# A fused attention, feed-forward and expert kernel: k and v loaded a chunk ahead, second group of their products in block 7; in the first chunk root and Relu read PSUM and the constants are made there; the last chunk's counts in block 9

## The chip, the cores and the metric

The kernel runs on one core of a Trainium2 chip. TensorE (PE in the rows) multiplies, VectorE (DVE), ScalarE (ACT) and GpSimd (POOL) work on elements, and SyncE (SP) issues most of the DMAs. Each engine works through its own queue in order, and engines wait for one another by semaphores. The metric is the device time in us of one execution, the median over runs.

## The reference

Three stages in float32. Attention without a softmax on q, k and v of (8 batches, 8 heads, 576 tokens, 64), a feed-forward layer 512 to 2048 to 512 with a leaky Relu (a slope alpha for each of the 2048 features), and a mixture of 8 experts (512 to 1024 to 512) of which each of the 4608 tokens takes one:

```python
kv = einsum('bhsd,bhse->bhde', k, v)
out = einsum('bhsd,bhde->bhse', q, kv)
x = out / sqrt(mean(out*out, -1) + 1e-6) * g_norm     # then tokens x 512
h = x @ w_in
x = (maximum(h, 0) + alpha * minimum(h, 0)) @ w_out
logits = x @ w_gate + modality_bias[modality_id]      # 8 experts
e = argmax(logits);  gate = softmax(logits)[e]
out = gate * (maximum(x @ w1[e], 0) @ w2[e])
```

## The kernel before

Tokens go through the first two stages in 12 chunks (c) of 384 tokens; a chunk has 16 blocks (s), one for each 128 hidden features. Every operand of the large products is split into a high and a low part and three products are summed. In block s TensorE does `first(c, s)` (12 products, h of block s into one of two PSUM banks), then `second(c, s - 1)` (9 products into the three banks of y). Between them lies the chain of a block: h is made into gg (a leaky Relu), ScalarE rounds gg to ghi, GpSimd subtracts and leaves glo, and `second` reads both. In chunk 0 gg is made by two Relus of ScalarE (L367, L368) and one VectorE operation (L369); there `cut` also splits the weights: ScalarE L162 and L184, VectorE L171 and L176, GpSimd's subtraction L185, two cuts in a block. In later chunks gg is two VectorE operations that read h in PSUM (L371, L372), and the time is used for the rest:

- the attention of the next chunk: a batch covers one and a half chunks. In chunks 0, 2, 3, 5, 6, 8 and 9 the next chunk needs a new batch; its k and v come in four parts, into two slots `kvt`, by `load_kv` on SP. `kv_mm` (L228) multiplies two parts in block 3 and two in block 6, `kv_evict` (L232 on ScalarE, then L233 on VectorE) copies the result to `kvbd`, `attend` uses it from block 8 on (9 in chunk 0). `rsqrt` is the root of the norm, by integer steps on VectorE (L302 to L309).
- the choice of expert for the chunk before: `dots` on VectorE (24 of them, spread over the blocks by DOTS, in the last chunk by LAST_DOTS), `choose`, whose last result is hb, `count` (two small products that read hb), `weigh`, `place`, `scatter` of the rows into DRAM.
- the split of the experts' weights into DRAM, a piece a block in blocks 0 to 11: `pre_hi` (ScalarE), `pre_lo` (GpSimd, L215), `pre_store` (SP, L219), `pre_load` (SP, L208).

After the last chunk's `place`, `leader` picks the expert with the most tokens, whose rows and weights are loaded first; then 41 tiles of 128 rows go through the experts, TensorE busy throughout. The order of the work is the order in which the code calls the functions; a queue never takes a later instruction first. `spare` and the pool of `other` are PSUM, `one` and `two` are SBUF.

Of the kernel before, what the change touches and what calls it, by code (L numbers as in the profile page):

```python
# [13 lines left out]
I32 = mybir.dt.int32  # L14
U32 = mybir.dt.uint32
AF = mybir.ActivationFunctionType
ALU = mybir.AluOpType
# [6 lines left out]
S = 576  # L24
E = 8
NB = 8
CT = 384
NCH = NTOK // CT
# [12 lines left out]
FAR = [(1, e) for e in range(E)] + [(2, 6), (2, 7)]  # L41
PLAIN = 3
EARLY = 4
KV_AT = (0, 1, 3, 4)
DOTS = (0, 2, 5, 8, 11, 14, 17, 20, 22, 24)
LAST_DOTS = (0, 2, 5, 8, 12, 15, 18, 21, 24)


@with_exitstack
def fused(ctx: ExitStack, tc, qT, kv, g2, wmoe, alpha, wgate, bias, modality, w12, out):  # L50
    nc = tc.nc
    V, A, G, PE, SP = nc.vector, nc.scalar, nc.gpsimd, nc.tensor, nc.sync
# [23 lines left out]
    nalpha = one.tile([128, NFB], F32, name="nalpha")  # L76
# [32 lines left out]
    def other(n=512):  # L109
        return (pools[1] if pools else ps_a).tile([128, n], F32, tag="a", name="a")  # L110
# [179 lines left out]
    def rsqrt(c, others=(), part=None):  # L290

        if part == 1:
            fill(rsqrt_t[c], others)
            return
        ms = ms_t[c]
        if c > 1:
            it = spare[:, 96:120].bitcast(I32)
        else:
            it = one.tile([128, 24], I32, tag="it", name="it")
        u = one.tile([128, 24], F32, tag="u", name="u")  # L300
        y = it.bitcast(F32)
        steps = [lambda: V.tensor_scalar(ms, ms, 1.0 / 64, 1e-6, ALU.mult, ALU.add),  # L302
                 lambda: V.tensor_single_scalar(it, ms.bitcast(I32), 1, ALU.logical_shift_right),
                 lambda: V.tensor_tensor(it, magic, it, ALU.subtract),
                 lambda: V.tensor_scalar(ms, ms, -0.5, None, ALU.mult)]
        for _ in range(3):
            steps += [lambda: V.tensor_tensor(u, y, ms, ALU.mult),
                      lambda: V.tensor_tensor(u, u, y, ALU.mult),
                      lambda: V.scalar_tensor_tensor(y, u, 1.5, y, ALU.add, ALU.mult)]  # L309
        ms_t[c] = y  # L310
        rsqrt_t[c] = steps[7:]
        fill(steps[:7] if part == 0 else steps, others)
# [44 lines left out]
    def first(c, fb, between=None):  # L357
        ps = bank(CT)

        steps = [(k, *p) for k in range(4) for p in ((0, xhi), (0, xlo), (2, xhi))]  # L360
        if c == fb == 0:
            steps.sort(key=lambda step: (step[1], step[2] is xlo))
        for i, (k, part, x) in enumerate(steps):
            PE.matmul(ps, w_at(fb, part)[:, k * 128:(k + 1) * 128], x[:, k, :], start=(i == 0), stop=(i == 11))  # L364
        gg = two.tile([128, CT], F32, tag="gg", name="gg")
        if c == 0:
            A.activation(gg, ps, AF.Relu)  # L367
            A.activation(pad[:, 0:CT], ps, AF.Relu, scale=-1.0)  # L368
            V.scalar_tensor_tensor(gg, pad[:, 0:CT], nalpha[:, fb:fb + 1], gg, ALU.mult, ALU.add)  # L369
        else:  # L370
            V.tensor_scalar(gg, ps, 0.0, alpha_sb[:, fb:fb + 1], ALU.min, ALU.mult)  # L371
            V.scalar_tensor_tensor(gg, ps, 0.0, gg, ALU.max, ALU.add)  # L372
        if between:
            between()
        ghi = two.tile([128, CT], F32R, tag="ghi", name="ghi")
        A.copy(ghi, gg)  # L376
        glo = two.tile([128, CT], F32R, tag="glo", name="glo")
        G.tensor_tensor(glo, gg, ghi.bitcast(F32), ALU.subtract)  # L378
        g_t[c, fb] = (ghi, glo)
# [385 lines left out]
    with tc.manual_schedule():  # L765
# [72 lines left out]

        for c in range(NCH):
            nxt = c + 1  # L840
            kvb = [b for b in range(NB) if nxt < NCH and (nxt * CT) // S <= b <= (nxt * CT + CT - 1) // S
                   and not (c * CT) // S <= b <= (c * CT + CT - 1) // S]
            for s in range(NFB):
                edge = s == NFB - 1
                between = None
                if edge and nxt < NCH:
                    between = lambda: [take_x(nxt, k) for k in range(2)]
                elif s == 0 and c > 0:
                    between = lambda: [second(c - 1, NFB - 1, (2,)), y_out(c - 1, 1), y_out(c - 1, 0)]
                if c == 0:  # L850
                    cut(between=lambda: first(c, s, between))
                else:
                    first(c, s, between)
                if c == 0:
                    later = []
                    cut(later if s in (AT + 3, AT + 4) else None)
                    if s in AHEAD:
                        cut()
                if s == 0 and c > 0:
                    y_out(c - 1, 2)  # L860
                n = (c - 1) * 12 + s
                if c > 0 and s < 12 and n < 128:
                    pre_hi(n)
                    pre_lo(n)
                    pre_store(n)
                    if n + 2 < 128:
                        pre_load(n + 2)
                if c == 1 and 2 <= s < 6:
                    constants(s - 2)
                if s > 0:  # L870
                    second(c, s - 1)
                if edge and nxt < NCH:
                    for k in range(2, 4):
                        take_x(nxt, k)
                    second(c, s, (0, 1))
                elif edge:
                    turn_rows(0)
                    second(c, s)

                if kvb and s in (3, 6):  # L880
                    kv_mm(kvb[0], s - 3 and 2)
                    kv_mm(kvb[0], (s - 3 and 2) + 1)
                if kvb and s in KV_AT:
                    load_kv(kvb[0], KV_AT.index(s))
                if kvb and s == 6:
                    kv_evict(kvb[0])
                if nxt < NCH:
                    at = AT if c == 0 else 8
                    if at < s <= at + 3:
                        squares(nxt, s - at - 1)  # L890
                    if at <= s < at + 3:
                        if s != at + 1:
                            attend(nxt, (0, 1) if s == at else (2,))
                        attended(nxt, s - at)
                    if s == 11 and nxt + 1 < NCH:
                        load_q(nxt + 1)
                    if c == 0 and s in (at + 3, at + 4):
                        rsqrt(nxt, later, s - at - 3)
                    if c > 0 and s == at + 3:
                        rsqrt(nxt)  # L900
                    if s == at + 4:
                        scale_x(nxt, 0)
                        scale_x(nxt, 1)
                        turn_x(nxt, 0)
                    if s == at + 5:
                        scale_x(nxt, 2)
                        turn_x(nxt, 1)
                        turn_x(nxt, 2)

                if c > 0:  # L910
                    at = LAST_DOTS if nxt == NCH else DOTS
                    if s + 1 < len(at):
                        dots(c - 1, at[s], at[s + 1])
                    end = len(at) - 2
                    if s == end:
                        choose(c - 1)
                    if s == end + 1:
                        count(c - 1)
                        weigh(c - 1)
                    if s == end + 2:  # L920
                        place(c - 1)
                        if nxt == NCH:
                            leader()
                            scatter(c - 1, range(3))
                    if nxt < NCH and end + 2 <= s < end + 5:
                        scatter(c - 1, [s - end - 2])
                    if nxt == NCH and s == 11:
                        load_rows(0)
                        load_expert(0, (0,))
                        load_rows(1)  # L930
                        load_rows(2)
                        load_expert(0, (1,))
                elif edge:
                    pre_load(0)
                    pre_load(1)
                    SP.dma_start(wg_sb.rearrange("p a b -> p (a b)"), wgate.rearrange("a b -> (a b)").partition_broadcast(128))
                    G.memset(pad, 0.0)
                    G.memset(pad[:, D + 1:D + 2].bitcast(I32), OOB)
                    for j in range(8):
                        SP.dma_start(xb[E * BUCKET + j * 128:E * BUCKET + (j + 1) * 128], pad)  # L940
# [107 lines left out]
```

## Time and profile before

| | us |
|---|---|
| median of 3 runs | 1377.96 (1376.11 to 1378.64) |
| the profiled execution | 1376.92 |
| its span, first to last instruction | 1375.3 |
| TensorE busy | 1343.8 (98%) |
| VectorE, GpSimd, ScalarE busy | 995.7, 666.6, 526.9 |

Chunk 0 lasts until 110.6 us, the chunks after it some 72 us each until 906, the experts from there to the end. A matmul's busy time is modelled, and matmuls are pipelined, so the share of TensorE is read together with its waits: a wait is the idle time in front of an instruction, put down to what released it. A timeline row merges equal instructions in a row, gives the start of the first, and in brackets the idle time before it.

### The profile page before, as it was taken

To read this page: it belongs to the slowest core of one execution; us is meant where nothing else is said; L and a number is where in the kernel's file an instruction comes from. 1 tells how busy PE (TensorE), PEld (TensorE's weight loads), DVE (VectorE), ACT (ScalarE), POOL (GpSimd) and SP (SyncE) were. 2 spreads that over 40 slices of the span, in tenths; PEclk is the share of its full clock that TensorE was granted. 3 is DMA by queue.
4 is the path that set the end of the run, shared out by engine and by line. 5 is a ranking of instruction groups with operands and counts; after the bars stand their busy time and mean duration, and the time that the engine had idled before them with its cause. 6 is when DMAs were issued, how large, how long until landed. Compare 5 with 4: busy or idle time off the path is not lost. (4 is left out here: it accounts for less than half of the span.)

```text
span 1375.3 us, 26710 instructions
## 1 busy us (share of the span) xinstructions
PE 1343.8 (98%) x8886; PEld 1155.8 (84%) x8886; DVE 995.7 (72%) x2204; ACT 526.9 (38%) x1147; POOL 666.6 (48%) x643
## 2 busy tenths in 40 slices
PE   8989999999999999999999999999999999999997
PEld 7778888889898888988888889888888888888886
DVE  5779877777877777877777787756666666666662
ACT  4773323232332323232333333143444445544442
POOL 2765655555655464746555565543333333333320
PEclk9999999999999999999999999999999999999999
DMA  8855645453536364446545353367511171637784
GB/s 287 293 186 163 221 153 187 164 197 130 193 137 232 116 232 159 163 160 218 174 164 200 120 194 106 123 253 252 178 52 52 51 288 49 244 102 304 302 325 168
DMA packets 88949, 250.69 MB, mean 182 GB/s; under 512 B 19245, under 2 KB 39213, under 8 KB 86640
## 3 DMA queue, kind: packets, MB, share of 16 engines
q1 hardware_dynamic: 77056, 220.82, 45.6%
q0 software_dynamic: 11760, 28.14, 6.2%
q8 instruction: 78, 1.28, 0.4%
q14 instruction: 55, 0.45, 0.1%
HBM read 158.69 MB, written 91.54 MB: 182 GB/s over the span
## 5 line engine op out<-in xcount | busy, mean ns | idle before, releaser
L364 PE MATMUL h<-xhi,W 128*128 128x384 f32 x1536 | 430.0, 341 | 1.3 <-POOL W L185 0.7
L378 POOL TENSOR_TENSOR glo<-gg,ghi 128x384 fp32r<-128x384 f32 x192 | 237.2, 1235 | 360.8 <-ACT ghi L376 341.7
L392 PE MATMUL y<-W,ghi 128*128 128x512 f32 x1152 | 300.5, 396 | 8.3 <-ACT ghi L376 7.4
L376 ACT CAST ghi<-gg 128x384 fp32r<-128x384 f32 x192 | 98.9, 515 | 517.5 <-DVE gg L372 219.4
L364 PEld LDWEIGHTS h<-xhi,W 128*128 128x128 f32 x1536 | 280.4, 188 | 12.4 <-ACT xhi L353 1.5
L364 PE MATMUL h<-xlo,W 128*128 128x384 f32 x768 | 257.9, 336 | 0.0
L392 PEld LDWEIGHTS y<-W,ghi 128*128 128x128 f32 x1152 | 213.8, 188 | 48.9 <-ACT ghi L376 12.7
L409 DVE CUSTOM_DVE_ANT_0 junk<-yrow,wg_sb 128x512 f32<-128x512 f32 x242 | 218.6, 903 | 8.7 <-ACT yrow L403 3.1
L654 PE MATMUL h<-W,xhi 128*128 (+1 forms) x656 | 206.4, 395 | 0.0
L654 PE MATMUL y<-W,hth 128*128 (+1 forms) x656 | 204.6, 393 | 1.3 <-DMA W<-wsp 1.0
L215 POOL TENSOR_TENSOR raw<-raw 128x512 f32<-128x512 f32 x128 | 197.9, 1546 | 0.2
L371 DVE TENSOR_SCALAR gg<-h,alpha_sb 128x384 f32<-128x384 f32 x176 | 108.2, 615 | 118.2 <-PE h L364 112.5
L731 POOL DMA_INDIRECT out_dram<-kvbd,tail x41 | 43.2, 1054 | 283.3 <-ACT kvbd L729 240.4
L392 PE MATMUL y<-W,glo 128*128 128x512 f32 x576 | 163.7, 393 | 0.0
L364 PEld LDWEIGHTS h<-xlo,W 128*128 128x128 f32 x768 | 144.3, 188 | 5.9 <-DVE xlo L354 0.2
L654 PEld LDWEIGHTS h<-W,xhi 128*128 128x128 f32 x656 | 122.7, 187 | 29.7
L654 PEld LDWEIGHTS y<-W,hth 128*128 128x128 f32 x656 | 123.0, 188 | 28.4 <-DVE lg L409 1.4
L654 PE MATMUL h<-W,xlo 128*128 (+1 forms) x328 | 129.2, 394 | 0.0
L392 PEld LDWEIGHTS y<-W,glo 128*128 128x128 f32 x576 | 108.3, 188 | 23.4 <-POOL glo L378 0.7
L654 PE MATMUL y<-W,htl 128*128 (+1 forms) x328 | 127.8, 390 | 0.0
L691 DVE TENSOR_SCALAR hh<-h 32x256 f32<-32x256 f32 x296 | 123.3, 416 | 4.6
L712 DVE TENSOR_TENSOR htl<-hh,hth 128x512 fp32r<-128x512 f32 x74 | 51.2, 692 | 100.1 <-ACT hth L711 100.1
(212 smaller groups left out, 1492.9 us busy)
## 6 DMA issues: line engine op xcount, KB each, us to landing
wsp<-raw SPq DMA_DIRECT2D x128, 512.0 KB, 3.0
W<-wsp SPq DMA_DIRECT2D x16, 4096.0 KB, 14.5
raw<-in_w_dram SPq DMA_DIRECT2D x128, 256.0 KB, 3.5
kvt<-in_kv_dram SPq DMA_DIRECT2D x30, 512.0 KB, 5.0
xs<-xb POOLq DMA_DIRECT2D x140, 64.0 KB, 2.5
raw<-in_wmoe_dram SPq DMA_DIRECT2D x17, 511.8 KB, 5.2
qT<-in_qT_dram SPq DMA_DIRECT2D x11, 768.0 KB, 7.9
wg_sb<-in_wmoe_dram SPq DMA_DIRECT2D x15, 511.8 KB, 5.8
```

The source lines that it names most:

```text
L215: G.tensor_tensor(lo, lo, hi, ALU.subtract)
L364: PE.matmul(ps, w_at(fb, part)[:, k * 128:(k + 1) * 128], x[:, k, :], start=(i == 0), stop=(i == 11))
L371: V.tensor_scalar(gg, ps, 0.0, alpha_sb[:, fb:fb + 1], ALU.min, ALU.mult)
L376: A.copy(ghi, gg)
L378: G.tensor_tensor(glo, gg, ghi.bitcast(F32), ALU.subtract)
L392: PE.matmul(y_t[c][t], a[:, t * 128:(t + 1) * 128], w, start=(fb == i == 0), stop=(fb == NFB - 1 and i == 2))
L409: V.tensor_tensor_reduce(spare if i >= 22 else junk, y, wg_sb[:, e, :], 1.0, 0.0, ALU.mult, ALU.add, lg_t[c][:, t, e:e + 1])
L654: m = PE.matmul(ps, a, w, start=start, stop=stop)
L691: m = V.tensor_scalar(to, of, 0.0, None, ALU.max) if mine else A.activation(to, of, AF.Relu)
L712: V.tensor_tensor(v, x, u.bitcast(F32), ALU.subtract)
L731: d = G.indirect_dma_start(out=out, out_offset=IndirectOffsetOnAxis(ap=tail[:, i, 1:2].bitcast(I32), axis=0), in_=y, in_offset=None, bound ...
```

## The change

Four edits. (1) `load_kv` of parts 0 and 1 moves from blocks 0 and 1 to blocks 12 and 13 of the chunk before (in chunk 0, which has none before it, it stays); parts 2 and 3 stay in blocks 3 and 4; the products of parts 2 and 3 and `kv_evict` move from block 6 to block 7. (2) In chunk 0 the positive Relu is written onto h itself in PSUM, and VectorE reads it there; the root that chunk 0 makes for chunk 1 keeps its iterate in PSUM. (3) The constants of parts 0 and 1 move from blocks 2 and 3 of chunk 1 to blocks 7 and 8 of chunk 0, parts 2 and 3 from blocks 4 and 5 of chunk 1 to blocks 9 and 10. (4) In the last chunk `count` moves from the end of block 8 to block 9, ahead of its `second`, and a dot moves from block 3 to block 0.

```diff
-KV_AT = (0, 1, 3, 4)
-LAST_DOTS = (0, 2, 5, 8, 12, 15, 18, 21, 24)
+LAST_DOTS = (0, 3, 6, 9, 12, 15, 18, 21, 24)
 def rsqrt
+        elif c == 1:
+            it = other(24).bitcast(I32)
 def first
         if c == 0:
-            A.activation(gg, ps, AF.Relu)
             A.activation(pad[:, 0:CT], ps, AF.Relu, scale=-1.0)
-            V.scalar_tensor_tensor(gg, pad[:, 0:CT], nalpha[:, fb:fb + 1], gg, ALU.mult, ALU.add)
+            A.activation(ps, ps, AF.Relu)
+            V.scalar_tensor_tensor(gg, pad[:, 0:CT], nalpha[:, fb:fb + 1], ps, ALU.mult, ALU.add)
 the loop over c and s
-            kvb = [b for b in range(NB) if nxt < NCH and (nxt * CT) // S <= b <= (nxt * CT + CT - 1) // S
-                   and not (c * CT) // S <= b <= (c * CT + CT - 1) // S]
+            kvb, kvn = ([b for b in range(NB) if n < NCH and (n * CT) // S <= b <= (n * CT + CT - 1) // S
+                         and not (n * CT - CT) // S <= b <= (n * CT - 1) // S] for n in (nxt, nxt + 1))
-                if c == 1 and 2 <= s < 6:
-                    constants(s - 2)
+                if c == 0 and s in (7, 8) or c == 1 and s in (9, 10):
+                    constants(s - 7)
+                if nxt == NCH and s == 9:
+                    count(c - 1)
                 if s > 0:
                     second(c, s - 1)
...
-                if kvb and s in (3, 6):
+                if kvb and s in (3, 7):
                     kv_mm(kvb[0], s - 3 and 2)
                     kv_mm(kvb[0], (s - 3 and 2) + 1)
-                if kvb and s in KV_AT:
-                    load_kv(kvb[0], KV_AT.index(s))
+                if kvb and c == 0 and s < 2:
+                    load_kv(kvb[0], s)
+                if kvb and s in (3, 4):
+                    load_kv(kvb[0], s - 1)
+                if kvn and s in (12, 13):
+                    load_kv(kvn[0], s - 12)
-                if kvb and s == 6:
+                if kvb and s == 7:
                     kv_evict(kvb[0])
...
                     if s == end + 1:
-                        count(c - 1)
+                        if nxt < NCH:
+                            count(c - 1)
                         weigh(c - 1)
```

The order on the engines. SP's queue from the last load of q in chunk 1 into chunk 2, before (raw: a piece of an expert's weights, wsp: its place in DRAM):

```order
L120 DMA qT_2637<-in_qT_dram 128x1536
L219 DMA wsp_80<-raw_2537 128x1024
L208 DMA raw_2825<-in_w12_dram 128x512
L128 DMA kvt_79<-in_kv_dram 128x4x256
L129 DMA kvt_79<-in_kv_dram 64x256
L219 DMA wsp_80<-raw_2625 128x1024
L208 DMA raw_2854<-in_w12_dram 128x512
L128 DMA kvt_79<-in_kv_dram 128x4x256
L129 DMA kvt_79<-in_kv_dram 64x256
```

and now:

```order
L119 DMA qT_2637<-in_qT_dram 128x1536
L127 DMA kvt_79<-in_kv_dram 128x4x256
L128 DMA kvt_79<-in_kv_dram 64x256
L127 DMA kvt_79<-in_kv_dram 128x4x256
L128 DMA kvt_79<-in_kv_dram 64x256
L218 DMA wsp_80<-raw_2537 128x1024
L207 DMA raw_2829<-in_w12_dram 128x512
L218 DMA wsp_80<-raw_2625 128x1024
L207 DMA raw_2856<-in_w12_dram 128x512
```

Both parts of kvt stand right behind q, and the stores, each of which waits for GpSimd, come after them; before, two of these stood ahead of part 1.

VectorE's queue in chunk 0 from the second cut of block 6 on, before (L171, L176: the cuts; L369: gg; L233: k and v copied out):

```order
L171 TENSOR_SCALAR spare<-wg_sb 128x512
L176 SCALAR_TENSOR_TENSOR yrow_90<-yrow_90,spare 128x512
L369 SCALAR_TENSOR_TENSOR gg<-pad,nalpha,gg 128x384
L171 TENSOR_SCALAR spare<-wg_sb 128x512
L176 SCALAR_TENSOR_TENSOR yrow_88<-yrow_88,spare 128x512
L233 COPY kvbd_101<-a 64x4x64
L171 TENSOR_SCALAR spare<-raw 128x512
L176 SCALAR_TENSOR_TENSOR yrow_89<-yrow_89,spare 128x512
L369 SCALAR_TENSOR_TENSOR gg<-pad,nalpha,gg 128x384
```

and now, from the second cut of block 7 on (L170 and L175 are the cuts, L370 is gg, L746, L751 and L752 are the constants):

```order
L170 TENSOR_SCALAR spare<-raw 128x512
L175 SCALAR_TENSOR_TENSOR yrow_90<-yrow_90,spare 128x512
L746 TENSOR_TENSOR bsel<-mod_sb,bias_sb 128x288
L232 COPY kvbd_101<-a 64x4x64
L170 TENSOR_SCALAR spare<-raw 128x512
L175 SCALAR_TENSOR_TENSOR yrow_88<-yrow_88,spare 128x512
L370 SCALAR_TENSOR_TENSOR gg<-pad,nalpha,h 128x384
L170 TENSOR_SCALAR spare<-wg_sb 128x512
L175 SCALAR_TENSOR_TENSOR yrow_89<-yrow_89,spare 128x512
L751 SCALAR_TENSOR_TENSOR junk<-mod_sb,bias_sb 128x288
L752 TENSOR_TENSOR bsel<-bsel,junk 128x288
```

gg reads h in PSUM in place of gg in SBUF; the copy stands a block later, and the constants stand between two cuts.

TensorE's queue in the last chunk, blocks 8 and 9, before:

```order
L392 MATMUL y<-W,ghi 128x512 x6
L392 MATMUL y<-W,glo 128x512 x3
L455 LDWEIGHTS tri
L455 MATMUL spare<-hb,tri 128x24
L456 LDWEIGHTS ones
L456 MATMUL spare<-hb,ones 128x24
L364 MATMUL h<-xhi,W 128x384
```

and now, from within the products of `first` of block 9:

```order
L365 MATMUL h<-xhi,W 128x384 x2
L365 MATMUL h<-xlo,W 128x384
L365 MATMUL h<-xhi,W 128x384
L456 LDWEIGHTS tri
L456 MATMUL spare<-hb,tri 128x24
L457 LDWEIGHTS ones
L457 MATMUL spare<-hb,ones 128x24
L393 MATMUL y<-W,ghi 128x512 x6
```

The counts (tri, ones) come behind `first` of block 9 and no longer ahead of it.

## Rows read from the trace of the kernel before

**Rows 1.** the page: its span, and busy us (share) of each engine.
```profile
span 1375.3 us, 26710 instructions
...
PE 1343.8 (98%) x8886; PEld 1155.8 (84%) x8886; DVE 995.7 (72%) x2204; ACT 526.9 (38%) x1147; POOL 666.6 (48%) x643
```

**Rows 2.** waits of TensorE, whole run: engine, line, releaser, us in total, times, longest.
```profile
PE a L228 <- DMA kvt<-in_kv_dram: 10.0, 9, 1.7
PE y L392 <- ACT ghi L376: 7.4, 6, 2.3
...
PE spare L455 <- DVE hb L436: 1.1, 1, 1.1
PE y L654 <- DMA W<-wsp: 1.0, 1, 1.0
```

**Rows 3.** timeline of TensorE, chunk 3: start us, us, instruction, idle before.
```profile
271.85 0.80 PE L228 MATMUL a<-kvt 128*64 128x64 f32 x20
273.94 0.80 PE L228 MATMUL a<-kvt 128*64 128x64 f32 x20 [1.29 <-DMA kvt<-in_kv_dram]
274.67 0.44 PE L364 MATMUL h<-xhi,W 128*128 128x384 f32 x1
...
287.35 1.39 PE L228 MATMUL a<-kvt 128*64 128x64 f32 x40
288.66 0.44 PE L364 MATMUL h<-xhi,W 128*128 128x384 f32 x1
```

**Rows 4.** waits of TensorE between 170 and 850 us.
```profile
PE a L228 <- DMA kvt<-in_kv_dram: 9.3, 8, 1.7
```

**Rows 5.** timeline of SP's queue, end of chunk 2 and chunk 3.
```profile
241.81 0.79 SPq L120 DMA_DIRECT2D qT<-in_qT_dram  x1
...
268.40 0.78 SPq L128 DMA_DIRECT2D kvt<-in_kv_dram  x1
```

**Rows 6.** timeline of chunk 0, GpSimd and VectorE in block 4.
```profile
46.04 2.55 POOL L185 TENSOR_TENSOR W<-yrow,W 128x512 fp32r<-128x512 f32 x2
...
47.92 1.08 DVE L369 SCALAR_TENSOR_TENSOR gg<-pad,nalpha,gg 128x384 f32<-128x384 f32 x1 [0.19 <-ACT pad L368]
```

**Rows 7.** the line of gg in chunk 0: ns min/median/max.
```profile
L369 DVE SCALAR_TENSOR_TENSOR gg<-pad,nalpha,gg x16: 577/971/1094, 27.7 to 107.4; 128x384 f32<-128x384 f32 x16
```

**Rows 8.** VectorE by line, 91 to 104 us: count, busy us, mean ns.
```profile
L307 DVE TENSOR_TENSOR u<-it,ms 128x24 f32<-128x24 f32 x3 | 2.5, 847 | 0.1
...
L309 DVE SCALAR_TENSOR_TENSOR it<-u,it 128x24 f32<-128x24 f32 x3 | 1.6, 535 | 0.1
...
L304 DVE TENSOR_TENSOR it<-magic,it 128x24 int32<-128x24 int32 x1 | 0.9, 866 | 0.0
...
L308 DVE TENSOR_TENSOR u<-u,it 128x24 f32<-128x24 f32 x3 | 0.5, 180 | 0.1
```

**Rows 9.** timeline of chunk 1, GpSimd and VectorE during the root.
```profile
164.64 1.29 POOL L215 TENSOR_TENSOR raw<-raw 128x512 f32<-128x512 f32 x1
...
165.18 0.19 DVE L309 SCALAR_TENSOR_TENSOR spare<-u,spare 128x24 f32<-128x24 f32 x1
```

**Rows 10.** timeline of chunk 1, a constant and the wait behind them.
```profile
121.59 0.45 DVE L745 TENSOR_TENSOR bsel<-mod_sb,bias_sb 128x288 f32<-128x288 int32 x1
...
133.43 0.96 PE L392 MATMUL y<-W,ghi 128*128 128x512 f32 x3 [1.13 <-ACT ghi L376]
```

**Rows 11.** timeline of chunk 2: hb ready, and the counts that read it.
```profile
226.65 0.18 DVE L436 CAST hb<-hot 128x24 bf16<-128x24 f32 x1
...
228.80 0.19 PE L455 MATMUL spare<-hb,tri 128*128 128x24 bf16 x1
```

**Rows 12.** timeline of VectorE, first blocks of the last chunk.
```profile
842.20 1.38 DVE L409 CUSTOM_DVE_ANT_0 junk<-yrow,wg_sb 128x512 f32<-128x512 f32 x1
...
843.51 0.61 DVE L371 TENSOR_SCALAR gg<-h,alpha_sb 128x384 f32<-128x384 f32 x1
```

**Rows 13.** timeline of SP's queue, the second half of the first expert's weights.
```profile
908.86 0.35 SPq L592 DMA_DIRECT2D W<-wsp  x1
```

## The prediction

> **What bounds the kernel now.** I read the page's busy times first: TensorE works 1343.8 us of a span of 1375.3, so 31.5 us in all can be won without making its products cheaper, and an edit counts only by what it takes out of TensorE's idle time [rows 1]. Next the waits of TensorE: 10.0 us in nine waits for k and v (the products of L228), 7.4 us in six for ghi (L392), 1.1 us once for hb (the counts, L455), 1.0 us once for the first expert's weights (L654) [rows 2]. The change touches the first three, and the fourth, as shown below, answers to the third. The other engines I read only where TensorE waits for them: VectorE is 72% busy, but in chunk 0 and in the last chunk it is behind.
>
> **k and v a chunk ahead.** Chunk 3 shows what goes. The products of part 0 start at 271.85, those of part 1 only at 273.94, 1.29 us of it being the wait, and the next block's product at 274.67: 2.82 us. The same 40 products at 287.35, whose data had landed, take until 288.66: 1.31 us. So a block with one such wait loses 1.51 us, the wait and 0.22 us of refilling [rows 3]. Chunks 2 to 9 have eight waits of 9.3 us in all [rows 4]; with 0.2 us each that is 9.3 + 1.6 = 10.9 us. Why the data is late: part 1 was issued at 268.40 and had landed by 273.94, 5.5 us later, but SP can't issue it sooner, since a store that waits for GpSimd stands ahead of it. In the new order it stands behind the load of q, which went out at 241.81, some 30 us before its use [rows 5]: covered several times over. Parts 2 and 3 keep their places at blocks 3 and 4; at 287.35 their products show no wait. Those products now come one block later, 12.7 us from 274.67 for three blocks or 4.2 us each, of which the lost wait takes back 1.5 [rows 3]. So no wait is due there.
> The price of the move is in kv_evict, which now stands in block 7. VectorE waits in its queue for the products and for ScalarE's copy; behind it stand dots, choose and hb, for which the counts wait. In chunk 2 hb was done at 226.65 and the counts came at 228.80: 2.0 us to spare [rows 11]. VectorE loses at block 7 the idle time that it had at block 6, and its blocks from there to hb are two shorter in dots (two dots a block in place of three), so I take the spare time to hold and the cost as nothing. Were it gone, each us would be paid in six chunks.
>
> **Chunk 0: Relu and root read PSUM.** L369 takes 577 ns at best, 971 in the median, 1094 at most [rows 7]. The cause stands beside it: at 47.92 it starts while two subtractions of GpSimd run from 46.04 to 48.59, and where 0.58 would have ended at 48.50 it ends at 49.00, 0.41 after GpSimd [rows 6]: an operation with two inputs in SBUF waits until GpSimd's is done. The steps of the root show the same: L307 takes 847 ns in the mean of three, L309 535, L304 866, against 180 for L308, which met an idle GpSimd [rows 8]. In chunk 1, where the root lies in PSUM, L309 takes 0.19 us at 165.18 inside a GpSimd subtraction that lasts from 164.64 to 165.93 [rows 9].
> On the shared ports the Trainium skill says the same (SBUF — State Buffer, Who interferes with whom): a VectorE instruction with two SBUF inputs contends with a GpSimd one that reads SBUF, and waits it out whole; with one SBUF input it doesn't. The trace agrees, 866 and 847 ns against 190.
> What is saved on VectorE: of the sixteen I take thirteen as held, at the median, 13 x (0.97 - 0.58) = 5.1 us [rows 7]; in the root 3 x (0.847 - 0.19) + 3 x (0.535 - 0.19) + 0.866 - 0.19 = 3.7 us [rows 8, 9]. Both lie in the chain from Relu over gg and ghi to TensorE. ScalarE's Relu onto PSUM is shown by no row. Nearest is VectorE: 190 ns into PSUM against 180 into SBUF for 24 columns [rows 8, 9]; 16 times as wide that is 0.16 us more a block, 2.6 us in chunk 0 as the upper end, and nothing (or a little gained) as the lower. I take nothing, since start and not width makes most of so short an operation. The bank of h is now held until L369 has read it, but TensorE needs it only after second of the same block, which waits for the later ghi: no cost.
> **The constants in blocks 7 and 8** stand in the same chain. Three VectorE operations of 0.45 us, all of two SBUF inputs (L745 is the first [rows 10]), come between the cuts, where GpSimd subtracts for about 2.6 us a block [rows 6]. Own time 1.4 us; each may wait out one subtraction of 1.29 us [rows 9], 3.9 us in all. So 1.4 to 5.3 us; I take 3.9, two of three held in full. Their GpSimd parts (a memset, a select, three iotas) I count as hidden where GpSimd waits for ghi; if not, glo comes later by them, within the range below.
> Chain of chunk 0: 5.1 + 3.7 - 3.9 = 4.9 us. The cap is what TensorE waits there: 7.4 - 1.1 for ghi (the sixth wait lies in chunk 1 [rows 10]), 10.0 - 9.3 for k and v (block 6, gone by the move to block 7), 7.0 us, and refilling [rows 2, 4]. I take 5.0 us for all of chunk 0, with 0.7 (k and v alone) and 8 as ends.
> **Chunk 1** loses the constants of blocks 2 and 3 and with them the wait of 1.13 us at 133.43 [rows 10]: with refilling 1.3 us. Parts 2 and 3 are small GpSimd work in blocks 9 and 10.
>
> **The last chunk's counts** stand one product group later, by which hb is done: 1.1 us less for TensorE there [rows 2]. I count it as nothing. After the first dots VectorE has no idle time: the dot of 842.20 ends as L371 starts at 843.51 [rows 12]. So hb, place, leader, the scatter, the first rows and the weights' second half (issued at 908.86 [rows 13]) come when VectorE is through, not when TensorE is, and TensorE waits 1.0 us for these weights already [rows 2]. What it wins at the counts it waits more there. One dot goes from block 3 to block 0: it may make VectorE 0.9 us sooner or later (a dot held takes 1.38 [rows 12]), and TensorE gains or loses with it. Range: 2.0 won (both waits gone) to 1.0 lost.
>
> **Sum.** 10.9 + 5.0 + 1.3 + 0 = 17.2 us. The profiled execution took 1376.92 us, 1.6 more than its span; 1376.92 - 17.2 = 1359.7. Its time is 1.0 under the median of the three runs, 1377.96, which spread from 1376.11 to 1378.64; I say 1360.
>
> **Rivals.**
> *The constants eat chunk 0's gain* (0.15). For it: all three are held and GpSimd's subtractions get in between them, 5.3 us, and the Relu takes its 2.6: 5.1 + 3.7 - 7.9 = 0.9, about the 0.7 of k and v. Against: not every one finds GpSimd at work, as none of the three did in chunk 1, where the first took 0.45 [rows 10]. Time: 1360 + 4.3 = 1364. By the Trainium skill's rule on the shared ports (named above), this is the part of the change that goes against its grain.
> *The counts are worth their wait* (0.12). For it: the moved dot lets VectorE reach hb sooner, so that the weights come sooner as well: 1.1 + 1.0. Against: VectorE has the same number of dots, back to back. Time: 1358.
> *The wait for k and v turns into one for ghi* (0.08). In blocks 4 to 6 VectorE had used TensorE's 1.3 us to catch up. Against: the chunks without these products have no ghi wait at all (eight waits between 170 and 850, all for k and v [rows 4]). Half of 10.9 lost: 1365.
> *No gain* (0.02): loads still behind a waiting store; the order shows them ahead of it. Within 0.2%, 1377.
> *Slower* (0.02): kv_evict in block 7 holds VectorE so long that hb is late in all six chunks that load k and v. It decides once VectorE loses more than the 2.0 us of [rows 11]; to end 3 us above today it must cost 17.2 + 3 over six chunks, 3.4 us each, so hb 5.4 us later than now. VectorE's wait would only have to move, not grow, and one block is 4.2 us: hardly. Time 1380.
>
> **Chances and range.** The forecast has 0.61. 0.2% is 2.75 us, about what a measurement of this kernel tells from no change. Faster by more: 0.61 + 0.15 + 0.12 + 0.08 = 0.96; within: 0.02; slower: 0.02. The likeliest case spans 1356 to 1363 by chunk 0 (0.7 to 8) and the last chunk (2.0 to -1.0) with the runs' scatter of 1 us. To take in the two neighbours I go from 1354 to 1366.
>
> **What will show it.** Right: no TensorE wait for k and v from chunk 1 on; L369's successor near 0.6 us throughout; root steps near 0.19; hb's wait gone in the last chunk and the wait for W grown towards 2 us. Each of the three constants' operations at 0.45 or held to 1.7 tells the first rival. Wrong: any hb wait in chunks 2 to 9, ghi waits in blocks 3 to 7 there, or as many us of ghi waits in chunk 0 as now.

## The result and the profile after

The changed kernel takes 1359.51 us (1359.27 to 1360.25) beside 1377.99 for the kernel before: ratio 0.9869, 95% interval [0.9852, 0.9886]. The forecast was 1360.

The profiled execution took 1359.29 us. The page, its span and busy times:

```profile
span 1357.7 us, 26718 instructions
PE 1339.8 (99%) x8886; PEld 1153.4 (85%) x8886; DVE 994.5 (73%) x2204; ACT 526.6 (39%) x1147; POOL 670.4 (49%) x643
```

The span fell by 17.6 us, TensorE's busy time by 4.0 [rows 1], so its idle time by 13.6. The waits of TensorE in the whole run:

```profile
PE y L393 <- ACT ghi L377: 5.5, 7, 1.6
PE h L793 <- POOL ident L779: 1.6, 1, 1.6
PE y L655 <- DVE lg L410: 1.2, 1, 1.2
```

Against [rows 2], the waits of the products of L227 (L228 before) for k and v and those of the counts for hb are gone. The 1.6 us at L793 lie in the first 22 us and were there before. The wait of 1.2 us at L655 stands where the one for the weights stood; lg is only the event that came last beside it (experiment 9 shows what it waits for). Of ghi's 7.4 us there are still 5.5, all but 0.3 of them in chunk 0.

Chunk 3 in TensorE's timeline, and in SP's queue the loads of its first two parts:

```profile
263.72 1.39 PE L227 MATMUL a<-kvt 128*64 128x64 f32 x40
265.04 0.44 PE L365 MATMUL h<-xhi,W 128*128 128x384 f32 x1
```
```profile
233.41 0.80 SPq L119 DMA_DIRECT2D qT<-in_qT_dram  x1
234.25 0.49 SPq L127 DMA_DIRECT2D kvt<-in_kv_dram  x1
...
235.60 0.60 SPq L127 DMA_DIRECT2D kvt<-in_kv_dram  x1
```

Where [rows 3] had 2.82 us for the 40 products, there are 1.32, and the loads stand right behind q's, 28 us ahead of their use.

Two things changed in chunk 0. The line of gg (ns min/median/max), and the three operations for the constants beside GpSimd's subtractions:

```profile
L370 DVE SCALAR_TENSOR_TENSOR gg<-pad,nalpha,h x16: 572/612/616, 27.4 to 103.0; 128x384 f32<-128x384 f32 x16
```
```profile
63.01 1.30 POOL L184 TENSOR_TENSOR W<-yrow,W 128x512 fp32r<-128x512 f32 x1
63.09 1.53 DVE L746 TENSOR_TENSOR bsel<-mod_sb,bias_sb 128x288 f32<-128x288 int32 x1
...
68.78 1.30 POOL L184 TENSOR_TENSOR W<-yrow,W 128x512 fp32r<-128x512 f32 x1
68.87 1.53 DVE L751 SCALAR_TENSOR_TENSOR junk<-mod_sb,bias_sb 128x288 f32<-128x288 int32 x1
...
70.35 1.27 POOL L184 TENSOR_TENSOR W<-yrow,W 128x512 fp32r<-128x512 f32 x1
70.43 1.51 DVE L752 TENSOR_TENSOR bsel<-bsel,junk 128x288 f32<-128x288 f32 x1
```

No gg is held any more (median 0.61 in place of 0.97, [rows 7]). Each of the three constants starts some 0.1 us behind a subtraction and ends 0.3 after it: all three are held, 4.57 us for what took 0.45 each in chunk 1 ([rows 10] shows the first, the others took 0.45 and 0.46).

One effect was not in the prediction's sum. The granted clock (PEclk, as a share of full speed) behind the root, in the kernel before and then at the same place after, and under each TensorE's first product there and the last of the next `first`:

```profile
core 0: us, PE busy (x) PEld busy (x) DVE busy (x) ACT busy (x) POOL busy (x), PEclk, DMA share, GB/s
99.00:101.80 2.80, 2.71 (x6) 2.16 (x7) 2.30 (x5) 2.52 (x6) 2.55 (x3) 0.50 1.13 470
```
```profile
99.09 2.93 PE L392 MATMUL y<-W,ghi 128*128 128x512 f32 x6 [2.33 <-ACT ghi L376]
...
104.70 0.34 PE L364 MATMUL h<-xhi,W 128*128 128x384 f32 x1
```
```profile
96.70:98.90 2.20, 2.14 (x9) 1.80 (x10) 1.57 (x7) 1.92 (x5) 1.98 (x2) 1.00 0.97 396
```
```profile
96.76 1.65 PE L393 MATMUL y<-W,ghi 128*128 128x512 f32 x6 [1.62 <-ACT ghi L377]
...
100.87 0.34 PE L365 MATMUL h<-xhi,W 128*128 128x384 f32 x1
```

Before, TensorE waited 2.33 us for ghi, and then its clock was at the lower of its two levels (0.50: 1.2 GHz): from that ghi product to the last product of the next `first` it took 99.09 to 104.70, 5.61 us, after the change 96.76 to 100.87, 4.11. So 1.5 us of the gain is the clock, which did not fall behind the shorter wait of 1.62.

**Where the 17.6 us came from**, from landmarks in the two traces: the product at 28 us that waits 0.73 us for W, the first product of chunk 1, the counts' first products in chunks 1 and 10, and the one of the same kind (a<-hb,tri) that comes once more among the first expert's products.

| stretch | before | after | won | forecast |
|---|---|---|---|---|
| start to 28 us | 28.26 | 27.96 | 0.3 | 0 |
| to chunk 1 | 82.36 | 78.27 | 4.1 | 5.0 |
| to the counts in chunk 1 | 43.47 | 41.86 | 1.6 | 1.3 |
| to the counts in chunk 10 | 655.81 | 644.01 | 11.8 | 10.9 |
| to the product with tri in the experts | 116.73 | 116.89 | -0.2 | 0 |

### The profile page after: what moved, and what is told of

Read it like the earlier page. It is cut to its first block, busy times and chain, and to the rows that moved or that the text cites. A ratio compares the mean times of both kernels' runs of the same rounds, so it can differ in the third digit from the quotient of the medians.

```text
span 1357.7 us, 26718 instructions
## 1 busy us (share of the span) xinstructions
PE 1339.8 (99%) x8886; PEld 1153.4 (85%) x8886; DVE 994.5 (73%) x2204; ACT 526.6 (39%) x1147; POOL 670.4 (49%) x643
## 5 line engine op out<-in xcount | busy, mean ns | idle before, releaser
L365 PEld LDWEIGHTS h<-xhi,W 128*128 128x128 f32 x1536 | 280.4, 188 | 12.4 <-ACT xhi L354 1.4
L655 PE MATMUL h<-W,xhi 128*128 (+1 forms) x656 | 206.4, 395 | 0.0
L655 PE MATMUL y<-W,hth 128*128 (+1 forms) x656 | 204.6, 393 | 1.6 <-DVE lg L410 1.2
L214 POOL TENSOR_TENSOR raw<-raw 128x512 f32<-128x512 f32 x128 | 203.3, 1588 | 0.1
L655 PEld LDWEIGHTS h<-W,xhi 128*128 128x128 f32 x656 | 122.6, 187 | 29.8
L655 PEld LDWEIGHTS y<-W,hth 128*128 128x128 f32 x656 | 123.1, 188 | 28.6 <-DVE lg L410 1.6
L655 PE MATMUL h<-W,xlo 128*128 (+1 forms) x328 | 129.2, 394 | 0.0
L655 PE MATMUL y<-W,htl 128*128 (+1 forms) x328 | 127.8, 390 | 0.0
```

The source lines that it names most:

```text
L214: G.tensor_tensor(lo, lo, hi, ALU.subtract)
L655: m = PE.matmul(ps, a, w, start=start, stop=stop)
```

## The experiments

**1. k and v alone.** The kernel before with `load_kv` a chunk ahead, parts 2 and 3 and kv_evict in block 7:

```
-                if kvb and s in (3, 6):
+                if kvb and s in (3, 7):
...
+                if kvn and s in (12, 13):
+                    load_kv(kvn[0], s - 12)
```

> The kernel before with the k and v edit alone. My theory (a wait that goes takes its refilling with it, and nothing takes its place): the eight waits of chunks 2 to 9 are worth what TensorE is ahead at the counts of chunk 10 over the counts of chunk 1, 17.8 - 6.0 = 11.8 us, and the wait in chunk 0 another 0.75 + 0.25 = 1.0: 12.8 us less, ratio 0.9907, about 1365 us; no wait for k and v from chunk 1 on. Rival (VectorE used these waits to catch up, so half comes back as waits for ghi): some 6 us less, 1372. In chunk 0 the wait of 2.3 us for ghi near 99 us and the granted clock near 0.58 behind it stay, since the root still lies in SBUF.

1365.89 us, ratio 0.9905 [0.9879, 0.9932], 12.4 less than the 1378.31 beside it. From the counts of chunk 1 to those of chunk 10, 644.14 us in place of 655.81: 11.7 won. Between 108 and 850 us two waits for ghi of 1.6 us in all are left, which the kernel before has too, so the rival's 6 us did not come back. In chunk 0 nothing was won: 82.38 in place of 82.36. A wait for ghi of 0.30 us took the place of the one for k and v, and by the start of chunk 1 nothing of the rest was left. The clock fell as before: the ghi products at 98.51 took 2.42 us where 1.65 is usual.

**2. PSUM alone.** The kernel before with root and Relu reading PSUM:

```
+        elif c == 1:
+            it = other(24).bitcast(I32)
...
+            A.activation(ps, ps, AF.Relu)
+            V.scalar_tensor_tensor(gg, pad[:, 0:CT], nalpha[:, fb:fb + 1], ps, ALU.mult, ALU.add)
```

> The kernel before with Relu and root reading PSUM in chunk 0, and nothing else. My theory: gg at 0.6 us, root steps at 0.19, so the wait of 2.3 us behind the root shrinks below 1.7 and the granted clock stays at 1.0 behind it, which is worth 1.5 us by itself; in all 4.4 (chunk 0 in the whole change) - 1.0 (k and v) + 1.0 (what the constants cost there) = 4.4 us less, ratio 0.9968, about 1373.6. Rival (the constants eat most of chunk 0's gain in the whole change): without them it is 7 us or more less, under 1371. Second rival (the chain is not the bound, the clock's fall comes from elsewhere): the clock still falls to about 0.58 and the gain stays under 2.5 us.

1370.20 us, ratio 0.9937 [0.9914, 0.9960]: 8.1 less, and chunk 0 takes 74.54 in place of 82.36, 7.8 won. The first rival's number came out, not mine: chunk 0 in the whole change is this large gain less a large price for the constants. The clock stayed at 1.00 behind the root, where TensorE waited 1.27 us.

**3. The constants back in chunk 1.**

```
-                if c == 0 and s in (7, 8) or c == 1 and s in (9, 10):
-                    constants(s - 7)
+                if c == 1 and 2 <= s < 6:
+                    constants(s - 2)
```

> The whole change, but the constants in blocks 2 to 5 of chunk 1 as before. My theory: in chunk 0 the waits for ghi behind blocks 8 and 9 (0.82 us, and part of 0.95) shrink, 1.0 us won; in chunk 1 the wait of 1.1 us comes back, 1.6 lost (what TensorE won between the start of chunk 1 and its counts, 6.0 - 4.4): 0.6 us slower than the whole change, about 1360.1, ratio 0.9873. Rival (all three operations are held to 1.5 us, 4.6 us in all, and TensorE waits for all of it): 4.6 - 1.4 - 1.6 = 1.6 us faster than the whole change, about 1357.9.

1358.30 us, ratio 0.9845 [0.9816, 0.9873]. Chunk 0 takes 74.51 in place of 78.27, 3.8 less; chunk 1 has its wait of 1.14 us back and takes 1.6 more. So in its new place this edit loses more than it wins: the span of the whole change is 1.5 us longer than this one's (3.8 less 1.6 is 2.2; the other 0.7 lies in stretches that the edit does not touch, 0.3 of it ahead of 28 us). The rival came out, with 1.2 us of its 1.6 in the medians.

**4. The counts back in block 8**, with the old dots:

```
-LAST_DOTS = (0, 3, 6, 9, 12, 15, 18, 21, 24)
+LAST_DOTS = (0, 2, 5, 8, 12, 15, 18, 21, 24)
...
-                if nxt == NCH and s == 9:
-                    count(c - 1)
...
-                        if nxt < NCH:
-                            count(c - 1)
+                        count(c - 1)
```

> The whole change, but the last chunk's counts in block 8 and its dots as before. My theory (VectorE, not TensorE, sets when the weights go out): the wait of 1.1 us for hb comes back, the wait of 0.3 us for ghi in block 0 goes, and the wait for the weights falls from 1.24 to about 1.0 or less: no difference, within 0.3 us of the whole change, about 1359.4, ratio 0.9866. Rival (the counts are worth their wait): 1.1 us or more slower, 1360.6 and up.

1359.70 us, ratio 0.9855 [0.9827, 0.9883], as the whole change. The wait for hb is back, the one for ghi in block 0 is gone, and the one for the weights is not shorter (I had said about 1.0 or less; this execution as a whole stood 1.0 us later than that of the changed kernel from the counts of chunk 1 on):

```profile
858.14 0.17 PE L456 MATMUL spare<-hb,tri 128*128 128x24 bf16 x1 [1.07 <-DVE hb L437]
...
904.58 0.71 PE L655 MATMUL y<-W,hth 128*128 128x512 f32 x2 [1.30 <-DMA W<-wsp]
```

**5. One input of the constants in PSUM.**

```
+        if part == 0:
+            bank_c[0] = other(324)
+            A.copy(bank_c[0][:, 288:324], mod_sb[:, :, 0])
+        if part < 2:
+            m = bank_c[0][:, 288:324].unsqueeze(2).to_broadcast(BA)
...
-            b2 = junk[:, 0:288].rearrange("p (a b) -> p a b", b=E)
+            b2 = bank_c[0][:, 0:288].rearrange("p (a b) -> p a b", b=E)
```

> The whole change, with one input of each of the constants' three VectorE operations in PSUM (ScalarE puts a copy of the modality there, and the second product goes there instead of to junk). My theory (they are held because both inputs lie in SBUF while GpSimd subtracts): each takes about 0.45 us in place of 1.53, VectorE has 3.2 us more in blocks 7 and 8 of chunk 0, the ghi wait of 0.82 us goes and chunk 1 starts near 103 us in place of 106.2, with no wait in chunk 1: about 3 us faster than the whole change, 1356.5. Rival (position, not the port: whatever stands between the cuts is late): the operations stay near 1.5 us and the time at 1359.5.

1356.88 us, ratio 0.9839 [0.9825, 0.9852], 2.6 under the changed kernel's 1359.51. The second and third of the operations at the same place:

```profile
68.41 1.30 POOL L184 TENSOR_TENSOR W<-yrow,W 128x512 fp32r<-128x512 f32 x1
68.50 0.46 DVE L757 SCALAR_TENSOR_TENSOR a<-a,bias_sb 128x288 f32<-128x288 f32 x1
68.99 0.45 DVE L758 TENSOR_TENSOR bsel<-bsel,a 128x288 f32<-128x288 f32 x1
```

Both run inside one subtraction of GpSimd's, at their own 0.45 us. It is the second SBUF input that held them, not the place. Chunk 0 takes 75.68, 2.6 less than in the changed kernel and 1.2 more than without the constants, near their own 1.4 us.

**6. Relu alone**: experiment 3 with the root of chunk 0 back in SBUF.

```
-        elif c == 1:
-            it = other(24).bitcast(I32)
```

> The whole change, with the root of chunk 0 back in SBUF and the constants back in chunk 1, so that of the PSUM edits Relu alone is left; to be read against the run with the constants back (1358.3). My theory: the root's steps are held again (0.5 to 0.87 us each, 3.7 us in all), the wait for ghi behind it grows from 1.2 to 2.3 us or so and the granted clock falls behind it again, 1.5 us: some 4 us slower than with the root in PSUM, 1362. Rival (the clock's fall in the kernel before came of all the waits of chunk 0 together, not of the one behind the root): the clock stays at 1.0 and the loss is under 2.5 us, 1360.5.

1360.37 us, ratio 0.9866 [0.9851, 0.9881]; chunk 0 takes 77.70, 3.2 more than in experiment 3 (the medians are 2.1 apart, the spans 2.4, since the stretch to 28 us was 0.6 shorter here). The wait behind the root, here and then in experiment 3, and the clock here, as expected:

```profile
93.82 2.04 PE L391 MATMUL y<-W,ghi 128*128 128x512 f32 x6 [2.34 <-ACT ghi L375]
```
```profile
93.36 1.65 PE L393 MATMUL y<-W,ghi 128*128 128x512 f32 x6 [1.24 <-ACT ghi L377]
```
```profile
93.80:97.00 3.20, 3.18 (x10) 2.53 (x11) 2.68 (x5) 2.52 (x5) 3.02 (x3) 0.67 1.07 449
```

From this product to the last of the next `first` it is 93.82 to 99.48, 5.66 us where an undisturbed clock takes 4.11: 1.55 for the clock. The longer wait is 1.1 (2.34 against 1.24), and the next one, 1.23 against 0.69, is 0.5 more: 3.2 in all. The waits for ghi in chunk 0 come to 4.5 us here and to 5.2 in the changed kernel, whose clock stayed, so their sum is not what the fall goes by, as the rival had it. My 4 us took more of VectorE's 3.7 us to reach TensorE than did.

**7. A dot less on VectorE** in the last chunk, its product by GpSimd in block 3 and its sum by ScalarE in block 5:

```
-LAST_DOTS = (0, 3, 6, 9, 12, 15, 18, 21, 24)
+LAST_DOTS = (0, 3, 6, 9, 12, 15, 18, 21, 23)
...
+                if nxt == NCH and s == 3:
+                    G.tensor_tensor(kvbd[1].rearrange("p a b -> p (a b)"), yb_t[c - 1][2][:, 0:D], wg_sb[:, 7, :], ALU.mult)
...
```

> The whole change, with the last of the 24 dots that VectorE does in the last chunk (the one of 1.33 us at the end of the row) multiplied by GpSimd and added up by ScalarE. My theory (VectorE's row of dots sets when the first expert's weights go out): hb is ready 0.7 to 1.4 us sooner (the dot goes, but GpSimd's product may hold another one by 0.7), the wait for the weights falls from 1.24 us to between 0 and 0.5: 0.8 us faster than the whole change, 1358.7. Rival (the weights wait for something else, the write of the spilled halves or the queue): no difference, 1359.5.

1360.07 us, ratio 0.9864 [0.9849, 0.9879]: nothing won. hb came no sooner (857.39 against 856.88, in a run that was 0.5 late from its start), since GpSimd's product, with two SBUF inputs, held the dots beside it:

```profile
840.67 1.78 POOL L872 TENSOR_TENSOR kvbd<-yrow,wg_sb 128x512 f32<-128x512 f32 x1
...
841.33 1.68 DVE L410 CUSTOM_DVE_ANT_0 junk<-yrow,wg_sb 128x512 f32<-128x512 f32 x1
...
843.04 1.38 DVE L410 CUSTOM_DVE_ANT_0 junk<-yrow,wg_sb 128x512 f32<-128x512 f32 x1
```

In the same block of the changed kernel two of three dots take 0.69. That is 1.0 us lost, and 0.8 more went in choose, where an operation of 0.18 us (L429) now took 1.01 while GpSimd subtracted. So this run tells nothing of what the weights wait for; experiment 9 had to.

**8. 5 and 7 together.**

> The constants with one input in PSUM and the moved dot together. My theory: the gains add, 3 + 0.8 = 3.8 us faster than the whole change, 1355.7. Rival (the chain of the first chunk has another bound once the constants are gone, as in the run with the constants back, where 2.9 us of waits for ghi were left): 2.5 us faster, 1357.

1357.21 us, ratio 0.9843 [0.9829, 0.9856]: as experiment 5 alone, since 7 gives nothing.

**9. VectorE's row made longer** in the last chunk:

```
                     if s == end:
+                        if nxt == NCH:
+                            for _ in range(4):
+                                V.tensor_copy(junk, spare)
                         choose(c - 1)
```

> The whole change, with four copies of 128x512 from PSUM (about 0.6 us each, results unused) added on VectorE between the last dot and choose in the last chunk: VectorE's row there is 2.4 us longer. My theory (the weights go out when VectorE is through): hb 2.4 us later, 0.5 us behind the place of its counts, so a small wait there, and the wait for the weights grows from 1.24 by the rest; both together 2.4 us more, 1361.9. Rival (TensorE's counts set it, so what stood 1.8 us ahead of them is spare): 0.5 us more, 1360. Second rival (the weights wait for the spilled halves to be written): no difference, 1359.5.

1361.18 us, ratio 0.9859 [0.9841, 0.9878]. The ratio is no larger than that of the change because the kernel before, measured beside it, took 1379.87 us here. In the profiled executions it took 2.06 us more than the changed kernel (1361.35 against 1359.29), 1.9 of it behind the counts of chunk 10. The chain in the changed kernel, on VectorE, SP and TensorE, and then in this one:

```profile
856.88 0.18 DVE L437 CAST hb<-hot 128x24 bf16<-128x24 f32 x1
...
891.25 0.35 SPq L593 DMA_DIRECT2D W<-wsp  x1
...
903.40 0.70 PE L655 MATMUL y<-W,hth 128*128 128x512 f32 x2 [1.24 <-DVE lg L410]
```
```profile
858.91 0.18 DVE L437 CAST hb<-hot 128x24 bf16<-128x24 f32 x1
...
893.35 0.35 SPq L593 DMA_DIRECT2D W<-wsp  x1
...
905.45 0.70 PE L655 MATMUL y<-W,hth 128*128 128x512 f32 x2
```

hb comes 2.03 us later, the second half of the weights goes out 2.10 later, and the products that read it start 2.05 later. From hb to the issue it is 34.4 us in both, in the kernel before 34.2 (874.68 to 908.86), in experiment 4 34.5; from the issue to the product 12.1 to 12.2 us in all four. The counts come 1.8 us behind hb in the changed kernel and 0.2 before, which changes the 34 us by 0.2 only. So VectorE sets this end of the chunk. I had named the wrong place for TensorE's wait: it came in block 9 for ghi (1.54 us), whose gg stands behind hb on VectorE, and it used up the later wait for the weights.

**10. The mean in PSUM too**, on top of experiment 5:

```
-                 lambda: V.tensor_scalar(ms, ms, -0.5, None, ALU.mult)]
+                 lambda: V.tensor_scalar(ms, mean, -0.5, None, ALU.mult)]
```

with `mean`, which the root's first step now writes, in the PSUM bank of the root.

> The constants with one input in PSUM, and the mean square of the root's first steps in PSUM too, so that the scaling by -0.5 (0.91 us, one input and its output in SBUF) reads PSUM. My theory (an operation from SBUF to SBUF is held by GpSimd as well, even with a single input): it takes 0.2 us, gg of that block comes 0.7 us sooner, the wait of 1.6 us for ghi falls to 0.9: 0.7 us faster than with the constants alone, 1356.2. Rival (it was late for the products of GpSimd's cut, and the next cut is late whatever stands ahead of it): no difference, 1356.9.

1356.37 us, ratio 0.9824 [0.9809, 0.9840]. The scaling in the changed kernel, and then here, each time while GpSimd subtracts:

```profile
91.91 2.55 POOL L184 TENSOR_TENSOR W<-yrow,W 128x512 fp32r<-128x512 f32 x2
...
92.32 0.92 DVE L306 TENSOR_SCALAR ms<-ms 128x24 f32<-128x24 f32 x1
```
```profile
88.93 2.56 POOL L184 TENSOR_TENSOR W<-yrow,W 128x512 fp32r<-128x512 f32 x2
...
89.55 0.18 DVE L308 TENSOR_SCALAR ms<-a 128x24 f32<-128x24 f32 x1
```

The wait for ghi in that block is 1.07 us in place of 1.60, and chunk 0 takes 75.15, 0.5 less. The medians of 10 and 5 differ by 0.5 us in the same direction, but their intervals overlap; the mechanism is shown, the gain in time hardly. It is the fastest version here, some 3 us under the changed kernel.

## Why the prediction was right

**k and v: right, a little small.** The eight waits of 9.3 us brought 11.8, not 10.9. The refilling was as said: the six groups of products of parts 0 and 1, with 8.75 us of these waits, took 18.15 us from their first product to the next `first` and take 7.88 now, so seven waits took 0.22 each with them. What the sum lacked is in the products of parts 2 and 3. I had looked at those of chunk 3 alone; four of the other five groups were late as well, three of them by 0.14 to 0.26 us with no wait shown and the one of chunk 9 by 0.74, and a block later, in the change, all six take 1.31 or 1.32. Chunk 8, before and after:

```profile
649.27 0.80 PE L228 MATMUL a<-kvt 128*64 128x64 f32 x20
...
650.84 0.45 PE L364 MATMUL h<-xhi,W 128*128 128x384 f32 x1
```
```profile
638.65 1.39 PE L227 MATMUL a<-kvt 128*64 128x64 f32 x40
639.96 0.44 PE L365 MATMUL h<-xhi,W 128*128 128x384 f32 x1
```

By the counts of chunk after chunk, those that load k and v are 1.5 to 2.7 us shorter, the three that don't (4, 7 and 10) by 0.04 at most. kv_evict in block 7 cost nothing, as said: no wait for hb in any chunk from 2 to 10. The 0.7 us that I counted for k and v in chunk 0 was nothing: there ghi was next (experiment 1).

**Chunk 0: right in its sum, in part by luck.** Relu: 4.7 us (82.38 of experiment 1 less 77.70 of experiment 6), said 5.1. The in-place Relu cost nothing (0.48 us, as into SBUF). Root: 3.2 (experiment 6 less 3), said 3.7. Constants: 3.8 (experiment 3), said 3.9. Sum 4.1, said 4.9. Two reasons behind these sizes were off. Of the constants I took two as held; all three are, 4.6 us on VectorE of which TensorE lost 3.8, so the sum fits by chance. And of the root's 3.2 about 1.5 is the clock, which the sum didn't have: by the way that I gave, VectorE's time reaching TensorE, the root brought 1.7 of the 3.7, and this size too fits by luck. The cap of 7.0 us by TensorE's waits was no cap for that reason: Relu and root together gave 7.8.

**Chunk 1** won 1.6, said 1.3: the wait of 1.13 took 0.5 of refilling with it.

**The last chunk's counts: right**, -0.2. VectorE's row sets when the weights go out (experiments 4 and 9). Against the kernel before, with both counted from the counts of chunk 10, TensorE lost 0.75 us in block 0, a wait of 0.26 for ghi in it; there the third dot now stands ahead of gg, and with the old dots (experiment 4) the loss is gone. At the counts it won 1.15, and around block 11 it lost 0.3, for which no wait stands in the rows. So it reached the first expert's products only 0.1 us sooner, and the weights went out 0.2 later: their wait grew from 0.97 to 1.24 and not towards 2 us.

**The rivals.** That the constants eat the gain was half true: all three are held, as it had it, but they cost 3.8 us and not 5.3, and Relu onto PSUM cost nothing. The counts were worth nothing, k and v did not turn into waits for ghi, hb was never late.

**The range** held the result, but its ends were not added up as written: chunk 0 from 0.7 to 8 and the last chunk from 2.0 to -1.0 give 1355 to 1365 for the likeliest case, not 1356 to 1363.

## What to carry to other kernels

Two VectorE operations of the same length cost 0.45 or 1.5 us by where their inputs lie: beside a busy GpSimd keep at most one tensor input in SBUF, and let an operation from SBUF to SBUF read PSUM. A moved edit is priced at its new place: the constants cost 1.6 us in chunk 1 and 3.8 in chunk 0, and came to 1.2 there once an input lay in PSUM. A wait that goes gives a little more than its length (0.2 us each here), unless the next one stands right behind it; one whose end another engine sets gives nothing.

## What was not expected of the hardware

After a wait of 2.3 us behind the root TensorE ran at a lower granted clock (0.50 and 0.67 in the two windows shown) in every kernel that had such a wait: before, experiments 1 and 6, for 1.5 to 1.6 us each time. After 1.1 to 1.6 us at the same place it stayed at 1.00 (the changed kernel, experiments 2 and 10), and so it did in experiment 2 behind a wait of 2.0 us for k and v near 407 us. What in or around the longer wait decides is not shown.

An operation with a single input from SBUF and its output in SBUF, 24 elements a partition, was held as well: 0.92 us against 0.18 from PSUM (experiment 10). The Trainium skill (SBUF — State Buffer, Who interferes with whom) has a rule for it: a tensor_scalar can enter a 2-port mode of VectorE, and in such a mode it contends with GpSimd. The two times agree with it; whether the scaling ran in that mode no row shows. The page frees an operation with one SBUF input only outside these modes, a condition that I had left out.
